# A fused attention and feed-forward kernel: the first stage with half loads on two queues and a second tile transposed by TensorE

## The chip, the cores and the metric

The kernel runs on one core of one Trainium2 chip. The metric is the device time of one execution in microseconds (us), taken as the median of several runs. Beside it stands one execution taken by the hardware profiler, whose trace gives every instruction's start and duration, in us from the start of its span.

## The reference

For an input `x` of 2048 rows and 640 columns, a linear-attention block and a gated feed-forward block are mixed by a gate for each row. Everything is bfloat16 at the boundaries.

```
qkv = x @ wqkv                       # 640 -> 3 * 640; 32 heads of 20
phi = lambda t: where(t > 0, t + 1, exp(t)) + 1e-6
pq, pk = phi(q), phi(k)
kv  = einsum("bhsd,bhse->bhde", pk, v);  z = sum over s of pk
o   = (pq @ kv) / (pq . z + 1e-6)
a   = o @ wo
b   = (gelu(x @ w_gate) * (x @ w_up)) @ w_down      # 640 -> 1728 -> 640
g   = sigmoid(sum(x * gate_w, -1))
out = g * a + (1 - g) * b
```

## The kernel before

Rows are cut into 16 tiles of 128 (`NT`), the 640 columns into five chunks of 128 (`KC`). `xT` holds x transposed (chunk by chunk, all rows) and is the stationary operand of the first stage; `x_aug` holds x as it lies. `wk` and `wq` are the k and q parts of `wqkv`, one resource for each chunk (`r_wk[k]`, `r_wq[k]`).

The instructions of every engine are written out by hand in program order. The class `_Plan` records each with the resources that it reads and writes, and puts a semaphore wait in front of an instruction for what it depends on. Each engine runs its own list in order, so an instruction that waits holds up all that follows it on its engine. Loads are issued by SP's queue (SyncE) or ACT's queue (ScalarE). A load that is issued with `dma_start_transpose` writes x transposed into `xT`; the others are plain.

The first stage runs as follows.

- POOL makes constants and the identity `ident` that TensorE's transposes need.
- ACT's queue issues a small load called touch (16 rows of 8 bytes), then wk1 and wk2 (`load_wk(1, "act")`), then an Exp on one column, which brings the table load, and then the gate vector `gw_sb`. SP's queue issues x tile 0 plain, wk0, `xT(1)` transposing, wk3, wk4, `xT(2)`, `xT(3)`, the five `wq`, `xT(4)` to `xT(15)`, and after these the rest of `x_aug` and the weights of the later stages.
- TensorE first runs matmuls on constants (`warm`, L425), then transposes tile 0 (`T`, L439; DVE copies the result out of PSUM, L443), and then works through pairs of matmuls for one tile and one chunk: `KM(n, ks)` (L459 and L460) multiplies by `wk`, `QM(n, ks)` (L474 and L475) by `wq`. `NXN` is the number of tiles that TensorE transposes, `NQ` the number of tiles that go through `KM` and `QM`; before these are 1 and 4.
- `gate_col` (L504) multiplies the gate vector by the identity, and DVE copies the five columns into column 640 of `wq` (L506, resource `r_gcol`); every `QM` reads it.
- `phi1` (ACT, L484 and L488) and `phi2` (DVE, L494 and L498) make pk and pq out of the PSUM banks of a `KM` or `QM`. `slot(n)` gives call n two of the eight banks.

From tile `NQ` on, `KQ(i)` (L545) does k and q of a tile in one pass of three groups of five matmuls, on banks 0 to 2 and 3 to 5 in turn. After the 16 tiles come `MM` (L602, L605), which multiplies pk with `x_aug`, the feed-forward groups `G` (L706), and the output stage (L827 to L880). The change leaves these as they are.

Of the kernel before, what the change touches and what calls it, by code (L numbers as in the profile page):

```python
# [15 lines left out]
NT = S // 128  # L16
KC = D // 128
# [3 lines left out]
EPS = 1e-6  # L21
XW = 656

NXN = 1
NQ = 4


class _Res:
# [134 lines left out]
def bass_gated_mix__linear_attn_block__geglu_ffn__prompt_kernel(  # L163
# [63 lines left out]
    with (  # L227
# [8 lines left out]
        with contextlib.ExitStack() as stack:  # L236
            dma_sems = [stack.enter_context(nc.semaphore("s_in%d" % i)) for i in range(n_dma_in)]

            P = _Plan(["pe", "act", "dve", "pool", "sp"])
# [9 lines left out]
            def new_dma_key():  # L249
                k = "in%d" % dma_next[0]  # L250
                dma_next[0] += 1
                return k
# [11 lines left out]
            x_aug = v16(R_XN, NT * XW).rearrange("p (i w) -> p i w", i=NT)  # L264
# [4 lines left out]
            wk = wkq[:, :, 0:640]  # L269
            wq = wkq[:, :, 640:1281]  # L270
# [31 lines left out]
            touch = v16(O_TOUCH, 16)  # L302
# [3 lines left out]
            r_xn = [P.sb("xn%d" % i, R_XN + i * XW, R_XN + (i + 1) * XW) for i in range(NT)]  # L306
# [3 lines left out]
            r_wk = [P.sb("wk%d" % k, R_WK + k * WW, R_WK + k * WW + 640) for k in range(KC)]  # L310
            r_wq = [P.sb("wq%d" % k, R_WK + k * WW + 640, R_WK + k * WW + 1280) for k in range(KC)]
# [30 lines left out]
            def dma_in(dst, src, writes, reads=(), eng="sp"):  # L342
                P.op(eng, lambda e, dst=dst, src=src: e.dma_start(dst, src),  # L343
                     reads=reads, writes=writes, dma=new_dma_key())

            def load_x(i, eng="sp"):
                dma_in(x_aug[:, i, 0:640], A_x[0, i * 128:(i + 1) * 128, :], [r_xn[i]], eng=eng)

            def load_wk(k, eng="sp", after=()):
                dma_in(wk[:, k, :], A_wqkv[k * 128:(k + 1) * 128, 640:1280], [r_wk[k]], reads=after, eng=eng)

            def load_xT(i, after=()):
                P.op("sp", lambda e: e.dma_start_transpose(xT[:, :, i * 128:(i + 1) * 128],  # L355
                                                           A_x[0, i * 128:(i + 1) * 128, :]),
                     reads=list(after), writes=[r_xT[i]], dma=new_dma_key())

            def load_wq(k, eng="sp"):
                dma_in(wq[:, k, 0:640], A_wqkv[k * 128:(k + 1) * 128, 0:640], [r_wq[k]], eng=eng)  # L360


            P.op("pool", lambda e: e.memset(ones32, 1.0), writes=[r_ones])
# [1 line left out]
                                                   base=0, channel_multiplier=1),  # L365
                 reads=[r_ones], writes=[r_ident])
            P.op("pool", lambda e: e.memset(v32(R_WO, NHC * 320), 0.0), reads=[r_ident], writes=[r_woz] + r_wo)
            P.op("act", lambda e: e.dma_start(touch[0:16, 0:4], A_wqkv[0:128:8, 640:644]),
                 writes=[P.res("touch")], dma=new_dma_key())
            load_x(0)  # L370
            load_wk(0)
            load_xT(1)
            load_wk(3)
            load_wk(4)
            load_wk(1, "act")
            load_wk(2, "act")

            zero = nc.const_aps.tensor(0.0, (128, 1), F32)
            P.op("act", lambda e: e.activation(eg[:, 0:1], zero, ACT.Exp), writes=[r_eg[0]])
            P.op("dve", lambda e: e.memset(gw_sb, 0.0), writes=[r_gw])  # L380
            dma_in(gw_sb[0:5, :], gate_w.rearrange("(k p) -> k p", p=128), [r_gw], eng="act")
            for i in range(2, NQ):
                load_xT(i)
            for k in range(KC):
                load_wq(k)
            for i in range(NQ, NT):
                load_xT(i)
            dma_in(x_aug[:, NXN:8, 0:640],
                   A_x[0, NXN * 128:8 * 128, :].rearrange("(i p) w -> p i w", p=128), r_xn[NXN:8])
# [5 lines left out]
            for h in range(2):  # L395
                src = A_wo[0:600, :].rearrange("(c h p) w -> h p c w", h=2, p=60)[h]
# [38 lines left out]
            def T(i, ks, tb):  # L435
                def fn(e):
                    last = None
                    for n, k in enumerate(ks):
                        last = e.transpose(psb[:, tb, n * 128:(n + 1) * 128],  # L439
                                           x_aug[:, i, k * 128:(k + 1) * 128], ident)  # L440
                    return last
                P.op("pe", fn, reads=[r_xn[i], r_ident], writes=[bank[tb]])
                P.op("dve", lambda e: e.tensor_copy(  # L443
                    xT[:, ks[0]:ks[-1] + 1, i * 128:(i + 1) * 128],
                    psb[:, tb, 0:len(ks) * 128].rearrange("p (k s) -> p k s", k=len(ks))),
                    reads=[bank[tb]], writes=[r_xTa[i] if ks[0] == 0 else r_xT[i]])
# [4 lines left out]
            def KM(n, ks):  # L451
                i = seq[n][1]
                b0, b1 = slot(n)

                def fn(e):
                    last = None
                    for k in ks:
                        lhs = xT[:, k, i * 128:(i + 1) * 128]
                        e.matmul(ps[:, b0, :], lhs, wk[:, k, 0:512], start=(k == 0), stop=(k == KC - 1))  # L459
                        last = e.matmul(ps[:, b1, 0:128], lhs, wk[:, k, 512:640],  # L460
                                        start=(k == 0), stop=(k == KC - 1))
                    return last
                P.op("pe", fn, reads=[r_xTa[i] if i < NXN and ks == [0] else r_xT[i]] + [r_wk[k] for k in ks],
                     writes=[bank[b0], bank[b1]])

            def QM(n, ks):
                i = seq[n][1]
                b0, b1 = slot(n)

                def fn(e):  # L470
                    last = None
                    for k in ks:
                        lhs = xT[:, k, i * 128:(i + 1) * 128]
                        e.matmul(ps[:, b0, :], lhs, wq[:, k, 0:512], start=(k == 0), stop=(k == KC - 1))  # L474
                        last = e.matmul(ps[:, b1, 0:129], lhs, wq[:, k, 512:641],  # L475
                                        start=(k == 0), stop=(k == KC - 1))
                    return last
                P.op("pe", fn, reads=[r_xT[i], r_gcol] + [r_wq[k] for k in ks],
                     writes=[bank[b0], bank[b1]])

            def phi1(n):
                b0, b1 = slot(n)
                m = n % 4
                P.op("act", lambda e: e.activation(e_buf[m], ps_flat[:, b0 * 512:b0 * 512 + 640], ACT.Exp),  # L484
                     reads=[bank[b0], bank[b1]], writes=[r_e[m]])
                kind, i = seq[n]
                if kind == "q":
                    P.op("act", lambda e: e.activation(eg[:, i:i + 1], ps[:, b1, 128:129], ACT.Tanh, scale=0.5),  # L488
                         reads=[bank[b1]], writes=[r_eg[i]])

            def phi2(n):
                b0, b1 = slot(n)
                m = n % 4
                P.op("dve", lambda e: e.tensor_scalar(e_buf[m], e_buf[m], 1.0, EPS, ALU.min, ALU.add),  # L494
                     reads=[r_e[m]], writes=[r_e[m]])
                kind, i = seq[n]
                dst, r_dst = (pk[i], r_pk[i]) if kind == "k" else (pq[i], r_pq[i])
                P.op("dve", lambda e: e.scalar_tensor_tensor(  # L498
                    dst, ps_flat[:, b0 * 512:b0 * 512 + 640], 1.0 + EPS, e_buf[m], ALU.add, ALU.max),
                    reads=[bank[b0], bank[b1], r_e[m]], writes=[r_dst])  # L500

            def gate_col():

                P.op("pe", lambda e: e.matmul(ps[:, 7, 0:5], gw_sb, ident[:, 0:5], start=True, stop=True),  # L504
                     reads=[r_gw, r_ident], writes=[bank[7]])
                P.op("dve", lambda e: e.tensor_copy(wq[:, :, 640:641], ps[:, 7, 0:5].unsqueeze(2)),  # L506
                     reads=[bank[7]], writes=[r_gcol])
# [4 lines left out]
            T(0, [0], 7)  # L512
            T(0, [1, 2, 3, 4], 6)
            warm(2, 128)
            for k in range(3):
                KM(0, [k])
            for k in range(3):
                KM(1, [k])
            KM(0, [3])
            KM(1, [3])  # L520
            gate_col()
            KM(0, [4])
            KM(1, [4])
            ALLK = list(range(KC))
            for n in range(2 * NQ):
                if n in (2, 3):
                    KM(n, ALLK)
                if n == NQ:
                    for k in ALLK:
                        QM(NQ, [k])  # L530
                        QM(NQ + 1, [k])
                if n > NQ + 1:
                    QM(n, ALLK)
                phi1(n)
                phi2(n)


            def KQ(i):
                b = 3 * (i % 2)
# [32 lines left out]
            for i in range(NQ, NT):  # L572
                KQ(i)
                if i == 4:
                    late_constants()
            P.op("dve", lambda e: e.tensor_scalar(gg, eg, 0.5, 0.5, ALU.mult, ALU.add),
                 reads=r_eg, writes=[r_g])
            P.op("dve", lambda e: e.tensor_scalar(omg, eg, -0.5, 0.5, ALU.mult, ALU.add),
                 reads=r_eg, writes=[r_omg])
# [365 lines left out]
```

## Time and profile before

| What | Value |
|---|---|
| Median of 3 runs | 273.34 us (273.16 to 273.55) |
| The profiled execution's own time | 273.49 us |
| Its span | 272.2 us |
| TensorE (PE) busy | 267.0 us, 98% of the span |
| VectorE (DVE) busy | 140.9 us, 52% |
| ScalarE (ACT) busy | 76.0 us, 28% |
| First L459 matmul, first L545 matmul | 4.45, 16.27 us |
| First matmul after the first stage (L612) | 48.94 us |

How to read the lines of a profile: PE is a TensorE matmul, PEld its weight load, which overlaps matmuls; SPq and ACTq are the DMA issues of SP's and ACT's queue, and their duration is the time of issuing, not of the transfer. A line of the timeline has the start, the duration (for several merged instructions, from the first start to the last end), engine, source line, operation, operands and count, and in brackets the engine's idle time before it and what ended it. Matmuls are pipelined: the shown duration of one is longer than the distance to the next one's start, which is what its work costs in a stream. The program's tiles all lie in one tensor named `pool`, and PSUM is `ps`.

### The profile page before, as it was taken

The numbers are of one execution on the slowest core, as the hardware profiler recorded it, in microseconds if no ns is written. First come the engines' busy times: TensorE is split into PE (matmuls) and PEld (weight loads), VectorE is DVE, ScalarE is ACT, GpSimd is POOL, SyncE is SP. The second block draws the span as 40 slices with busy tenths as digits, with TensorE's granted clock in tenths as the row PEclk, the third lists the DMA queues.
The fourth block names the chain that finished last, engine by engine and source line by source line (L and its number), as shares of the span: only waits on it lengthen the run. The fifth ranks groups of instructions, "written<-read, shape, count | busy, mean of one in ns | idle before, by whom it ended". The sixth has DMA issues, their size and how long they took to land.

```text
span 272.2 us, 3462 instructions
## 1 busy us (share of the span) xinstructions
PE 267.0 (98%) x1366; PEld 127.2 (47%) x1392; DVE 140.9 (52%) x248; ACT 76.0 (28%) x132; POOL 30.6 (11%) x30
## 2 busy tenths in 40 slices
PE   7999999999999999999999999999999999999997
PEld 3555555544445454444444444444444444444444
DVE  1678989997234335999999999634110000000200
ACT  2455555210422453332222232224011122121021
POOL 6000000003240002242332421000000000000000
DMA  7976999610200011614121221262031110110221
GB/s 192 203 117 120 356 401 379 117 3 19 58 19 2 23 52 48 198 28 52 24 48 29 46 48 25 60 233 94 2 78 40 39 39 19 41 39 19 58 60 39
DMA packets 42680, 23.61 MB, mean 87 GB/s; under 512 B 32167, under 2 KB 41255, under 8 KB 42535
## 3 DMA queue, kind: packets, MB, share of 16 engines
q1 hardware_dynamic: 42333, 23.05, 32.2%
q10 hardware_dynamic: 330, 0.33, 0.4%
q8 instruction: 11, 0.18, 0.3%
q14 instruction: 6, 0.05, 0.1%
HBM read 13.67 MB, written 2.63 MB: 60 GB/s over the span
## 4 chain that ended last, share of the span: by engine, by line
PE 96%; DMA 1%; SPq 1%; issue 1%; DVE 0%
PE ps L706 41%; PE ps L880 23%; PE ps L545 12%; PE ps L602 6%; PE ps L859 4%; PE ps L684 2%; PE ps L474 2%; PE ps L827 2%; PE ps L605 1%; DMA pool<-in_A_x_dram 1%; PE ps L459 1%; PE ps L840 1%; SPq L343 1%; SPq L355 0%; PE ps L755 0%
## 5 line engine op out<-in xcount | busy, mean ns | idle before, releaser
L706 PE MATMUL ps<-pool 128*128 128x512 bf16 x509 | 112.8, 379 | 0.7 <-issue 0.2
L706 PEld LDWEIGHTS ps<-pool 128*128 128x128 bf16 x520 | 50.6, 98 | 60.3
L880 PE MATMUL ps<-pool 128*128 128x512 bf16 (+2 forms) x300 | 62.2, 366 | 0.5 <-issue 0.2
L712 ACT ACTIVATE pool<-ps 128x512 f32<-128x512 f32 x52 | 31.1, 597 | 72.8 <-PE ps L706 70.1
L714 DVE TENSOR_TENSOR pool<-ps,pool 128x512 bf16<-128x512 f32 x52 | 34.7, 688 | 31.1 <-PE ps L706 29.8
L880 PEld LDWEIGHTS ps<-pool 128*128 128x128 bf16 x306 | 29.2, 98 | 33.4 <-issue 0.4
L863 DVE TENSOR_TENSOR pool<-ps,pool 128x512 bf16<-128x512 f32 x4 | 2.8, 692 | 61.5 <-PE ps L859 59.4
L545 PE MATMUL ps<-pool 128*128 128x512 bf16 (+1 forms) x176 | 32.5, 343 | 0.2
L770 POOL TENSOR_TENSOR pool<-pool 128x640 f32<-128x640 bf16 x16 | 22.5, 1406 | 72.6 <-DVE pool L772 65.8
L887 ACT ACTIVATE pool<-ps,pool 128x512 bf16<-128x512 f32 (+1 forms) x16 | 10.9, 681 | 68.6 <-PE ps L880 68.6
L545 PEld LDWEIGHTS ps<-pool 128*128 128x128 bf16 x180 | 17.6, 98 | 15.0
L564 DVE SCALAR_TENSOR_TENSOR pool<-ps,pool 128x128 bf16<-128x128 f32 (+2 forms) x36 | 21.7, 603 | 2.1
L555 ACT ACTIVATE pool<-ps 128x640 bf16<-128x640 f32 x24 | 16.9, 704 | 15.8 <-DVE pool L564 9.3
L602 PE MATMUL ps<-pool 128*128 128x512 bf16 x76 | 19.2, 379 | 0.1
L780 DVE TENSOR_TENSOR pool<-pool 128x640 bf16<-128x640 bf16 x16 | 13.2, 825 | 0.6
L778 DVE TENSOR_SCALAR pool<-pool 128x32 f32<-128x32 f32 x16 | 12.8, 802 | 0.6
L772 DVE TENSOR_REDUCE pool<-pool 128x32 f32<-128x640 f32 x16 | 12.9, 807 | 0.0
L650 DVE TENSOR_TENSOR pool<-pool 128x640 f32<-128x640 f32 x14 | 11.6, 825 | 0.5
L859 PE MATMUL ps<-pool 128*128 128x512 bf16 x51 | 11.4, 379 | 0.0
L652 POOL PARTITION_ALL_REDUCE pool<-pool x1 | 4.0, 3972 | 60.2 <-DVE pool L650 60.2
L602 PEld LDWEIGHTS ps<-pool 128*128 128x128 bf16 x78 | 6.9, 98 | 7.3
L561 DVE TENSOR_SCALAR pool<-pool 128x640 bf16<-128x640 bf16 x24 | 7.8, 326 | 1.7 <-ACT pool L555 0.4
(73 smaller groups left out, 123.4 us busy)
## 6 DMA issues: line engine op xcount, KB each, us to landing
out_dram<-pool SPq DMA_DIRECT2D x19, 128.0 KB, 1.7
pool<-in_B_w_gate_dram SPq DMA_DIRECT2D x1, 2080.0 KB, 14.3
pool<-in_B_w_up_dram SPq DMA_DIRECT2D x1, 2080.0 KB, 18.4
pool<-in_A_wqkv_dram SPq DMA_DIRECT2D x8, 160.0 KB, 3.0
pool<-in_A_x_dram SPq DMA_DIRECT2D x1, 1280.0 KB, 9.3
pool<-in_A_x_dram SPq DMA_DIRECT2D x1, 1120.0 KB, 6.4
pool<-in_B_w_down_dram SPq DMA_DIRECT2D x1, 1120.0 KB, 6.2
pool<-omg_row SPq DMA_DIRECT2D x1, 1024.0 KB, 4.8
```

Source lines behind the costliest of these rows:

```text
L545: last = e.matmul(ps[:, b + p, 0:c1 - c0], xT[:, k, i * 128:(i + 1) * 128], wkq[:, k, c0:c1], start=(k == 0), stop=(k == KC - 1))
L555: P.op("act", lambda e: e.activation(e_buf[m], ps_flat[:, o:o + 640], ACT.Exp), reads=banks, writes=[r_e[m]])
L564: P.op("dve", lambda e, c0=c0, c1=c1: e.scalar_tensor_tensor(dst[:, c0:c1], ps_flat[:, o + c0:o + c1], 1.0 + EPS, e_buf[m][:, c0:c1], ALU. ...
L602: last = e.matmul(ps[:, b, :], pk[i][:, c * 128:(c + 1) * 128], x_aug[:, i, 0:512], start=(i == 0), stop=(i == NT - 1))
L706: last = e.matmul(ps[:, b, :], w[:, k, fc * 128:(fc + 1) * 128], xT[:, k, j * 512:(j + 1) * 512], start=(k == 0), stop=(k == KC - 1))
L712: P.op("act", lambda e: e.activation(ge[n], ps[:, gb, :], ACT.Gelu_apprx_tanh), reads=[bank[gb]], writes=[r_ge[n]])
L714: P.op("dve", lambda e: e.tensor_tensor(hT[fc][:, j * 512:(j + 1) * 512], ps[:, ub, :], ge[n], ALU.mult), reads=[bank[ub], r_ge[n]], write ...
L770: P.op("pool", lambda e: e.tensor_tensor(tmp[n], pq[i], z_b, ALU.mult), reads=[r_pq[i], r_zb], writes=[r_tmp[n]])
L772: P.op("dve", lambda e: e.tensor_reduce(den[n], tmp[n].rearrange("p (h d) -> p h d", h=32), AX.X, ALU.add), reads=[r_tmp[n]], writes=[r_de ...
L780: P.op("dve", lambda e: e.tensor_tensor(pq[i].rearrange("p (h d) -> p h d", h=32), pq[i].rearrange("p (h d) -> p h d", h=32), den[n].unsqu ...
L859: last = e.matmul(ps[:, b, :], wd[:, fc, 512:640], hT[fc][:, j * 512:(j + 1) * 512], start=False, stop=(fc == NFC - 2), skip_group_check=True)
L880: last = e.matmul(ps[:, pb, 0:c1 - c0], lhs, rhs, start=False, stop=(q == len(rows) - 1), skip_group_check=True)
```

## The change

- `NXN` becomes 2 and `NQ` 2: TensorE transposes x tiles 0 and 1, and only tiles 0 and 1 go through `KM` and `QM`; `KQ` starts at tile 2.
- A new function `halves` loads rows 0 to 63 of a destination by SP's queue and rows 64 to 127 by ACT's queue, on one semaphore; a reader waits for both. x tile 1, the five `wk` and the five `wq` are loaded so. x tile 0 stays one load on SP's queue.
- The order of the loads is x0, wk0, x1, wk1, wk2, the gate vector (ACT's queue alone), wk3, wk4, wq0 to wq4, and then all transposing loads, from `xT(2)` on. The touch load is gone. The Exp with its table load stands ahead of ACT's loads.
- On TensorE, `T(1)` follows `KM(0, [0])`, with a DVE copy of all five chunks in one; then `KM(1, [0])`, then `KM` of tiles 0 and 1 in turn for each further chunk, with `gate_col` ahead of the last. Then `QM` of tiles 0 and 1 in turn (calls 2 and 3).

```diff
-NXN = 1
-NQ = 4
+NXN = 2
+NQ = 2
...
+            def halves(dst, src, r):
+                key = new_dma_key()
+                for h, eng in enumerate(("sp", "act")):
+                    d, f = dst[64 * h:64 * h + 64], src[64 * h:64 * h + 64]
+                    acc = P.op(eng, lambda e, d=d, f=f: e.dma_start(d, f),
+                               writes=[r] if h == 0 else [], dma=key)
+                r.writer = acc
...
-            P.op("act", lambda e: e.dma_start(touch[0:16, 0:4], A_wqkv[0:128:8, 640:644]),
-                 writes=[P.res("touch")], dma=new_dma_key())
-            load_x(0)
-            load_wk(0)
-            load_xT(1)
-            load_wk(3)
-            load_wk(4)
-            load_wk(1, "act")
-            load_wk(2, "act")
-
             zero = nc.const_aps.tensor(0.0, (128, 1), F32)
             P.op("act", lambda e: e.activation(eg[:, 0:1], zero, ACT.Exp), writes=[r_eg[0]])
             P.op("dve", lambda e: e.memset(gw_sb, 0.0), writes=[r_gw])
+            dma_in(x_aug[:, 0, 0:640], A_x[0, 0:128, :], [r_xn[0]])
+            load_wk(0)
+            load_x(1)
+            load_wk(1)
+            load_wk(2)
             dma_in(gw_sb[0:5, :], gate_w.rearrange("(k p) -> k p", p=128), [r_gw], eng="act")
-            for i in range(2, NQ):
-                load_xT(i)
+            load_wk(3)
+            load_wk(4)
             for k in range(KC):
                 load_wq(k)
-            for i in range(NQ, NT):
+            for i in range(NXN, NT):
                 load_xT(i)
...
-            for k in range(3):
+            KM(0, [0])
+            T(1, [0, 1, 2, 3, 4], 5)
+            KM(1, [0])
+            for k in range(1, KC):
                 KM(0, [k])
-            for k in range(3):
+                if k == KC - 1:
+                    gate_col()
                 KM(1, [k])
-            KM(0, [3])
-            KM(1, [3])
-            gate_col()
-            KM(0, [4])
-            KM(1, [4])
             ALLK = list(range(KC))
-            for n in range(2 * NQ):
-                if n in (2, 3):
-                    KM(n, ALLK)
-                if n == NQ:
-                    for k in ALLK:
-                        QM(NQ, [k])
-                        QM(NQ + 1, [k])
-                if n > NQ + 1:
-                    QM(n, ALLK)
+            phi1(0)
+            phi2(0)
+            phi1(1)
+            phi2(1)
+            for k in ALLK:
+                QM(2, [k])
+                QM(3, [k])
+            for n in (2, 3):
                 phi1(n)
                 phi2(n)
```

More of the change, by code (lines that the diff above doesn't have):

```diff
@@ L344, in dma_in, with load_x, load_wk @@
                      reads=reads, writes=writes, dma=new_dma_key())
[L348 to L352, printed above, removed]
+            def halves(dst, src, r):
[5 more added lines that the diff above has]
+                r.writer = acc
+            def load_x(i):
+                halves(x_aug[:, i, 0:640], A_x[0, i * 128:(i + 1) * 128, :], r_xn[i])
+            def load_wk(k):
+                halves(wk[:, k, :], A_wqkv[k * 128:(k + 1) * 128, 640:1280], r_wk[k])
             def load_xT(i, after=()):
@@ L357, in load_xT, with load_wq @@
                      reads=list(after), writes=[r_xT[i]], dma=new_dma_key())
-            def load_wq(k, eng="sp"):
-                dma_in(wq[:, k, 0:640], A_wqkv[k * 128:(k + 1) * 128, 0:640], [r_wq[k]], eng=eng)
+            def load_wq(k):
+                halves(wq[:, k, 0:640], A_wqkv[k * 128:(k + 1) * 128, 0:640], r_wq[k])
             P.op("pool", lambda e: e.memset(ones32, 1.0), writes=[r_ones])
```

## The prediction, made before the changed kernel ran

> **What bounds the kernel now.** I read the page first: one engine, TensorE, is busy for nearly the whole span, and the chain that ended last is TensorE too.
>
> ```profile
> span 272.2 us, 3462 instructions
> ...
> PE 267.0 (98%) x1366; PEld 127.2 (47%) x1392; DVE 140.9 (52%) x248; ACT 76.0 (28%) x132; POOL 30.6 (11%) x30
> ...
> PE 96%; DMA 1%; SPq 1%; issue 1%; DVE 0%
> ```
>
> So the time is the start of TensorE's stream, plus the work in it, plus its gaps. Next comes the chain in order of time: its last step that is no TensorE work is a transposing load of x; after it the chain stays on TensorE to the end, but for pieces of "issue".
>
> ```profile
> 4.15 3.90 DMA pool<-in_A_x_dram
> 8.05 0.05 issue
> 8.10 0.39 PE ps L459
> ```
>
> This is `xT(2)` (issued 4.15), for which `KM(2)` waited. The timeline of the first 17 us shows the gaps before that.
>
> ```profile
> 3.02 0.74 PE L439 MATMUL ps<-pool 128*128 128x128 bf16 x5
> ...
> 3.37 0.23 DVE L443 COPY pool<-ps 128x128 bf16<-128x128 bf16 x1 [2.39 <-PE ps L439]
> ...
> 3.79 0.42 DVE L443 COPY pool<-ps 128x512 bf16<-128x512 bf16 x1 [0.20 <-PE ps L439]
> ...
> 4.45 0.43 PE L459 MATMUL ps<-pool 128*128 128x512 bf16 x1 [0.48 <-DMA pool<-in_A_wqkv_dram]
> ...
> 5.90 0.39 PE L459 MATMUL ps<-pool 128*128 128x512 bf16 x1 [0.42 <-DMA pool<-in_A_x_dram]
> ```
>
> Real work begins at 4.45, when wk0 has landed (the copy it also needs ended at 3.60). Starts of pairs are 0.272 apart (8.10 to 10.82 for ten pairs of L459 and L460), so the fourth pair was due at 5.31 and came at 5.90 (0.59 lost, to `xT(1)`), and `KM(2)` was due at 7.83 and came at 8.10 (0.27 lost). Tile 4 (`KQ(4)`, L545) starts at 16.27. From there both kernels run the same program, and L545's matmuls had 0.2 us of idle time in all. **The change is therefore worth what it does to this 16.27**, as long as no later wait opens.
>
> The queue of SP, from the timeline of that engine:
>
> ```profile
> 0.79 0.40 SPq L343 DMA_DIRECT2D pool<-in_A_x_dram  x1
> 1.25 0.41 SPq L343 DMA_DIRECT2D pool<-in_A_wqkv_dram  x1
> 1.71 1.31 SPq L355 DMA_TRANSPOSE pool<-in_A_x_dram  x1
> 3.06 1.05 SPq L343 DMA_DIRECT2D pool<-in_A_wqkv_dram  x2
> 4.15 2.52 SPq L355 DMA_TRANSPOSE pool<-in_A_x_dram  x2
> 6.72 2.48 SPq L343 DMA_DIRECT2D pool<-in_A_wqkv_dram  x5
> 9.24 16.18 SPq L355 DMA_TRANSPOSE pool<-in_A_x_dram  x12
> ```
>
> A plain load costs its queue 0.40 to 0.57, a transposing one 1.2 to 1.7. Issue to landing: x0 2.2, wk0 3.1, the five wq 2.6 to 3.2, transposing loads 3.0 to 4.4.
>
> **Part 1: what is removed.** The waits for `xT(1)` (0.59) and `xT(2)` (0.27 at this place) and the touch load go. The touch was ACT's first issue (0.42 from 0.78); wk0's second half takes its slot. At most 0.86 is returned here, and up to 0.68 more if work could start at 3.77, where the two last warming matmuls end (0.107 each, after the transposes' 3.55).
>
> **Part 2: the Exp that now stands first on ACT.** In the timeline its table load ran from 2.20 to 3.48, and ACT's next DMA, behind it in program order, was issued at 2.27. The issue did not wait, so I take 0. If it did, all second halves would come up to 1.28 later; no row speaks for that.
>
> **Part 3: wk0 and x1 in halves.** No row shows a half load this early. Bounds for wk0: a load with little beside it landed 2.2 after its issue (x0), one with company 3.1. Its later half is SP's, issued at 1.25: landing 3.45 to 4.35. x1's halves are issued at about 1.7: landing 3.9 to 4.8. In quarter-microsecond windows DMA moved 159 and 133 GB/s from 1.75 to 2.25, SP's queue almost alone, with the engines half idle; with both queues full it moved 384, 389 and 362 from 3.25 to 4.0. So a second queue helps until about 370. x0, wk0 and x1 are 0.49 MB, which before had passed by 3.75; with ACT's queue carrying bulk from about 2.0 this should be some 3.4 to 3.6. x0's own last packets (2.5) came about 0.5 before its landing, wk0's (about 3.6) 0.7. I take wk0 at 3.8 and x1 at 4.4, nearer the middle.
>
> The Trainium skill ("DMA: Bandwidth & Descriptors", Rules for kernel authors) speaks against this part: two transfers to disjoint partition halves are not worth it, since both spread over the same 16 engines. By it wk0 stays near 4.4 and the sum below ends 0.3 higher; the half-idle engines before 2.25 speak for some gain, the ceiling of 390 after 3.25 for the rule.
>
> **Part 4: TensorE transposes x1, and `KM(1,[0])` waits for it.** `T(1)` adds five transposes and a copy, and everything on TensorE stands behind `KM(1,[0])`, because its queue runs in order: `KM(0,[1])`, whose data are there, cannot pass. Steps: `KM(0,[0])` starts at 3.85. TensorE is still slow there: L439's 128-column matmuls have 311 ns up to 3.55, L460's 219 from 4.72, and the 512-column one at 4.45 had 429 against 379, so the change fell about 0.1 after 4.45. At the slow pitch (0.427 for 512 columns, 0.107 for 128) the pair ends at 4.4. The transposes take 0.53 all slow, 0.28 all fast; with the change near 4.55, 0.37: to 4.77. The last result comes about 0.16 later. The copy of 640 columns, from 225 ns for 128 and 424 for 512, is 0.49: from 4.95 to 5.44. `KM(1,[0])` starts at 5.5. Bounds: 5.2 (loads at the short latency, clock change before 4.0) and 5.8 (x1 at 4.8; the copy then ends at 5.74). The idle stretch of about 0.75 takes the place of the two removed.
>
> The Trainium skill ("TensorE: Matmul & The Clock Gate", Part 1) calls the window of the clock gate free-running, so the change of clock need not fall at 4.55 again; by its half-microsecond scatter `KM(1,[0])` would move by about a quarter, an estimate from that page.
>
> **Part 5: gate column.** `gate_col` moves from three microseconds before its first reader to one pair before it. It started at 7.27 and its DVE copy ended at 7.68, 0.41 later; the next reader now is due 0.06 + 0.27 = 0.33 after it. With a hop of 0.06 that is 0.14 of wait. Bounds: 0 and 0.2.
>
> **Part 6: wk1 to wk4, wq.** SP's half loads follow at 0.46 each; ACT's, with the gate vector's 0.57 between, put the last half of wk3 at 3.3, of wk4 at 3.75, wq0 at 4.2, wq4 at 6.0. With 3.1 to landing: 6.4, 6.9, 7.3 and 9.1; needed at about 6.9, 7.4, 8.1 and 10.3. Cost 0, with 0.5 in hand; a wk4 that landed 4.0 after its issue would cost 0.4.
>
> **Part 7: transposing loads behind.** SP passes twelve plain issues before `xT(2)`: 0.79 + 0.46 for x0 + 11 x 0.46 to 0.55 = 6.3 to 7.3 instead of 4.15. Landing (3.0 to 4.1 after): 9.3 to 11.4; I take 6.5 + 3.9 = 10.4, as `xT(2)` itself took. `KQ(2)` is due at 5.5 + nine pairs 2.45 + gate 0.06 + 0.14 + ten pairs of 0.273 = 10.88. Cost 0, cover 0.5. Later ones come every 1.35, against 2.72 that a tile takes on TensorE. Tiles 2 and 3 in `KQ` cost (48.94 - 16.27) / 12 = 2.72 each, against 2.725 for ten pairs: nothing. Banks: `KQ(2)` needs what the first phi gives back some 1.8 after the last KM pair (8.0 to 9.68 in the timeline), and starts 2.9 after it: nothing. Big loads move by under 0.1 and are not waited for.
>
> **The sum.** `KQ(4)` starts at 10.88 + 2 x 2.72 = 16.32, against 16.27: +0.05. The profiled execution took 273.49 (span 272.2 and 1.29 around it), 0.15 above the median of 273.34, and all three runs lie within 0.39. So 273.54 in its terms, 273.4 in the median's. 0.2%, about what a measurement can tell from no change, is 0.55 us.
>
> **Rivals.** *Halves bring nothing* (the change doesn't do what it says): wk0 near 4.4, x1 at 4.8, `KM(1,[0])` at 5.8, +0.35: 273.7. For: 3.1 to landing in every load with company. Against: engines half idle before 2.25. *Slower: `xT(2)` behind twelve issues.* At 0.57 + 0.05 an issue (wk3's, the longest of these before) it starts at 8.1 and lands at 12.0 to 12.2, 1.2 late: 274.6. It decides from a landing at 10.9, and costs 0.2% from about 11.4. For: a wait on a transposing load ended last before. Against: most issues took 0.40 to 0.46. *Faster: short latency.* wk0 at 3.45, fast clock by 3.8, no gate wait: pair 3.77 to 4.04, transposes to 4.32, copy 4.48 to 4.97, `KM(1,[0])` at 5.03, `KQ(4)` at 15.7: -0.55, 272.8. Against: x1 would have to be there at 4.04, and the clock changed later.
>
> **Numbers.** Forecast (-0.25 to +0.3) 0.45; halves bring nothing 0.2; late `xT(2)` 0.2; short latency 0.15. Of the first two nearly all is within 0.2%, of the third nearly all slower, of the fourth nearly all faster: faster 0.14, same 0.63, slower 0.23. The range takes in the forecast, the halves' rival and the near parts of the others: 272.75 to 274.15.
>
> **What would show it.** Right: first L459 before 4.2; a wait of about 0.75 on L443's copy before the second pair; no wait on a transposing load before tile 2; first L545 near 10.9. Wrong: a wait on `in_A_x_dram` before L545; first L459 still at 4.4; the ACT queue's first issue after its table load; waits on wk or wq.

## The result, and the profile after

| | Median | Span of the profiled execution | First L545 matmul (tile 2 after, tile 4 before) | First matmul after the stage (L612) |
|---|---|---|---|---|
| Before | 273.44 us (4 runs) | 272.2 | 16.27 | 48.94 |
| Changed | 274.90 us (4 runs, 274.85 to 275.09) | 273.6 | 12.22 | 50.30 |

The changed kernel is slower: ratio 1.0056, 95% interval 1.0039 to 1.0074, or 1.5 us. The forecast was 273.4, no difference, with 272.75 to 274.15 as its range; the measured time lies above it. The ratios here and below leave out executions over 1.5% above the fastest of their kernel: 478 us once each in two experiments (the changed kernel's loads with the copy covered, and with fillers), 277.8 and 278.2 in a third (whole loads with the copy covered).

The chain of work that ended last is still almost all TensorE's, but what releases it early on has changed. First its line on the page (shares of the span), then its pieces in order of time (start, length, what).

```profile
PE 97%; DMA 1%; ACTq 1%; DVE 0%; issue 0%
```

```profile
4.29 0.51 ACTq L352
4.83 0.62 ACTq L352
5.48 3.48 DMA pool<-in_A_wqkv_dram
9.09 0.38 PE ps L477
...
12.22 38.08 PE ps L545 x210
```

L352 is the issue in `halves`. Before, the last release by a load in this chain was a transposing load of x, at 8.10. Now it is a half of wq0 that ACT's queue issued at 5.48, after other halves; the first `QM` waited for it until 9.09. (Two shorter waits behind it, ending at 10.92 and 12.22, are not told apart in the chain; the timeline has them.) From 12.22 the 14 tiles of `KQ` run through at 2.72 each, as before. So the whole loss is made before 12.22: 48.94 became 50.30, 1.36 us later, and the spans differ by 1.4.

The timeline shows where (L462 is the first matmul of a `KM` pair, L477 of a `QM` pair, L442 the transposes, L446 their copy, PEld the weight load of the matmul that waits):

```profile
4.24 0.38 PE L462 MATMUL ps<-pool 128*128 128x512 bf16 x1 [0.18 <-DMA pool<-in_A_wqkv_dram]
...
4.52 0.45 PE L442 MATMUL ps<-pool 128*128 128x128 bf16 x5
...
5.01 0.49 DVE L446 COPY pool<-ps 128x640 bf16<-128x640 bf16 x1 [0.70 <-PE ps L442]
5.56 0.10 PEld L462 LDWEIGHTS ps<-pool 128*128 128x128 bf16 x1 [0.76 <-DVE pool L446]
...
7.06 0.10 PEld L462 LDWEIGHTS ps<-pool 128*128 128x128 bf16 x1 [0.30 <-DMA pool<-in_A_wqkv_dram]
...
8.13 0.10 PEld L462 LDWEIGHTS ps<-pool 128*128 128x128 bf16 x1 [0.69 <-DMA pool<-in_A_wqkv_dram]
...
9.06 0.10 PEld L477 LDWEIGHTS ps<-pool 128*128 128x128 bf16 x1 [0.52 <-DVE pool L509]
...
10.92 0.10 PEld L477 LDWEIGHTS ps<-pool 128*128 128x128 bf16 x1 [0.37 <-DMA pool<-in_A_wqkv_dram]
...
12.19 0.77 PEld L545 LDWEIGHTS ps<-pool 128*128 128x128 bf16 x5 [0.34 <-issue]
```

The second pair comes at 5.56, as foretold. After it five waits follow. Counted from when the stream was due (the start of the last 128-column matmul plus 0.055), they are 0.14 for wk3, 0.52 for wk4, 0.37 for wq0 and the gate column, 0.20 for wq3, and 0.20 for `xT(2)`, which was issued at 8.38 and landed 3.7 later (12.09): 1.43 in all, where the prediction had 0.14. (For the last the profile names no releaser; the landing, 0.13 ahead of the matmul, fits.) The queues show why:

```profile
2.49 5.85 SPq L352 DMA_DIRECT2D pool<-in_A_wqkv_dram  x9
...
4.29 4.40 ACTq L352 DMA_DIRECT2D pool<-in_A_wqkv_dram  x7
...
8.38 3.95 SPq L363 DMA_TRANSPOSE pool<-in_A_x_dram  x3
```

Nine half loads took 5.85 us of SP's queue and seven 4.40 of ACT's: 0.65 and 0.63 each, for 82 kB. A whole load of 164 kB cost 0.40 to 0.58 before. The two queues together bring 164 kB in 0.64 us, so at most some 256 GB/s, and issue without a pause until 8.4 and 8.7.

### The profile page after: what moved, and what is told of

Read it like the earlier page. It is cut to its first block, busy times and chain, and to the rows that moved or that the text cites. A ratio compares the mean times of both kernels' runs of the same rounds, so it can differ in the third digit from the quotient of the medians.

```text
span 273.6 us, 3493 instructions
## 1 busy us (share of the span) xinstructions
PE 269.5 (98%) x1387; PEld 127.2 (46%) x1387; DVE 142.0 (52%) x251; ACT 76.0 (28%) x132; POOL 30.6 (11%) x30
## 4 chain that ended last, share of the span: by engine, by line
PE 97%; DMA 1%; ACTq 1%; DVE 0%; issue 0%
PE ps L706 41%; PE ps L880 23%; PE ps L545 14%; PE ps L602 6%; PE ps L859 4%; PE ps L827 2%; PE ps L684 2%; PE ps L605 1%; DMA pool<-in_A_wqkv_dram 1%; PE ps L477 1%; PE ps L428 1%; PE ps L840 1%; PE ps L755 0%; ACTq L352 0%; PE ps L731 0%; ACTq L343 0%
## 5 line engine op out<-in xcount | busy, mean ns | idle before, releaser
L706 PEld LDWEIGHTS ps<-pool 128*128 128x128 bf16 x520 | 50.6, 98 | 60.2
L880 PEld LDWEIGHTS ps<-pool 128*128 128x128 bf16 x306 | 29.1, 98 | 33.5 <-issue 0.4
L545 PE MATMUL ps<-pool 128*128 128x512 bf16 (+1 forms) x210 | 38.1, 344 | 0.0
L545 PEld LDWEIGHTS ps<-pool 128*128 128x128 bf16 x210 | 20.5, 98 | 17.7 <-issue 0.3
L564 DVE SCALAR_TENSOR_TENSOR pool<-ps,pool 128x128 bf16<-128x128 f32 (+2 forms) x42 | 25.3, 603 | 2.4
L555 ACT ACTIVATE pool<-ps 128x640 bf16<-128x640 f32 x28 | 19.7, 704 | 18.1 <-DVE pool L564 10.9
L602 PEld LDWEIGHTS ps<-pool 128*128 128x128 bf16 x78 | 7.0, 98 | 7.3
L561 DVE TENSOR_SCALAR pool<-pool 128x640 bf16<-128x640 bf16 x28 | 9.2, 327 | 1.7 <-ACT pool L555 0.2
```

Source lines behind the costliest of these rows:

```text
L545: last = e.matmul(ps[:, b + p, 0:c1 - c0], xT[:, k, i * 128:(i + 1) * 128], wkq[:, k, c0:c1], start=(k == 0), stop=(k == KC - 1))
L555: P.op("act", lambda e: e.activation(e_buf[m], ps_flat[:, o:o + 640], ACT.Exp), reads=banks, writes=[r_e[m]])
L564: P.op("dve", lambda e, c0=c0, c1=c1: e.scalar_tensor_tensor(dst[:, c0:c1], ps_flat[:, o + c0:o + c1], 1.0 + EPS, e_buf[m][:, c0:c1], ALU. ...
L602: last = e.matmul(ps[:, b, :], pk[i][:, c * 128:(c + 1) * 128], x_aug[:, i, 0:512], start=(i == 0), stop=(i == NT - 1))
L706: last = e.matmul(ps[:, b, :], w[:, k, fc * 128:(fc + 1) * 128], xT[:, k, j * 512:(j + 1) * 512], start=(k == 0), stop=(k == KC - 1))
L880: last = e.matmul(ps[:, pb, 0:c1 - c0], lhs, rhs, start=False, stop=(q == len(rows) - 1), skip_group_check=True)
```

## The experiments

Thirteen runs, in four groups, each group on one chip with its own runs of the kernel before; between groups only the ratios compare. All keep the changed kernel's TensorE program unless a diff shows otherwise.

**Does the issue cost lie in the half, or in two queues at once?**

Both halves on SP's queue:

```diff
-                for h, eng in enumerate(("sp", "act")):
+                for h, eng in enumerate(("sp", "sp")):
```

> The same 64-row halves, both on SP's queue, one after the other; ACT's queue has the gate vector alone. It measures what one half costs a queue with no other queue issuing. If the cost lies in the 64-row shape: 0.5 to 0.6 each, as the two 64-row loads of w_down before the output stage (0.59, 0.50). If it lies in two queues issuing at once: 0.40 to 0.43. Either way 22 issues in a row make the time longer than the changed kernel's: the first transposing load is issued near 11 (0.43) to 14 (0.55), and tile 2 waits to 15 to 18: 278 to 281 us.

One execution: 281.08 us. The view of L352 (duration in ns: least, median, most; first and last start):

```profile
L352 SPq DMA_DIRECT2D pool<-in_A_wqkv_dram x20: 561/597/601, 1.2 to 14.6; - x20
```

With no bulk on the other queue a half still costs 0.6. Then halves by columns, on both queues:

```diff
-                    d, f = dst[64 * h:64 * h + 64], src[64 * h:64 * h + 64]
+                    d, f = dst[:, 320 * h:320 * h + 320], src[:, 320 * h:320 * h + 320]
```

> Halves by columns instead of rows: 128 rows of 320 columns, the left half on SP's queue, the right half on ACT's. Same number of issues and bytes on both queues as the changed kernel; only the shape differs. If the cost lies in the 64-row shape: issues of 0.40 to 0.46, the first transposing load near 6.3, time near 273.7. If it lies in two queues issuing at once: issues of 0.6, 274.9. Rows of 640 bytes may also move more slowly than rows of 1280; then loads land later with short issues.

```profile
L352 ACTq DMA_DIRECT2D pool<-in_A_wqkv_dram x10: 353/453/454, 0.8 to 6.1; - x10
L352 SPq DMA_DIRECT2D pool<-in_A_wqkv_dram x10: 414/432/434, 1.3 to 6.0; - x10
```

Same bytes and number of issues, and both queues busy, but 0.43 to 0.45 each. So the cost belongs to the 64-row shape and not to two queues at once: both halves of that question are settled. The time was no better: 276.17, ratio 1.0075 (1.0040 to 1.0109). Rows of 640 bytes moved slowly at first (0.83 MB from 1.5 to 5.5 us, as with row halves), x1 came late (transposes at 5.39), and TensorE's clock was slow until 9.9 (512-column matmuls of 0.61 to 0.63). No load was waited for after x1.

**Whole loads in the same order.** In turn on both queues, and all on SP's:

```diff
-            def halves(dst, src, r):
-                key = new_dma_key()
...
+            qn = [0]
+
+            def halves(dst, src, r):
+                eng = "act" if qn[0] % 2 == 0 else "sp"      # second kernel: eng = "sp"
+                qn[0] += 1
+                dma_in(dst, src, [r], eng=eng)
```

> Whole loads of 128 rows in the same order of use, in turn on ACT's and SP's queue (wk0 ACT, x1 SP, wk1 ACT, ...); TensorE's program as in the changed kernel. Theory (the number and the cost of the half loads' issues is the loss: a half costs its queue 0.60 to 0.66 us, a whole one 0.41): issues go back to 0.40 to 0.46, SP comes to the first transposing load near 3.6 us instead of 8.38, the waits on wk3, wk4, wq3 and xT(2) go, and KQ starts tile 2 near 11.0 instead of 12.22: about 1.2 us less than the changed kernel, 273.7, the kernel before's time within 0.3. Rival 1 (two queues that issue at the same time slow each other): issues stay at 0.6, but there are half as many; wk4 still lands before 7.0, so the time is also near 273.7, and the issue rows tell it apart. Rival 2 (the DMA engines' rate is the limit, about 230 GB/s): wk4 and wq land as late as with halves, and the time stays at 274.9.

> Whole loads in order of use, all on SP's queue, ACT's queue with the gate vector alone. Theory: an issue costs 0.41 to 0.43, pitch 0.47; the first transposing load is issued near 0.79 + 12 x 0.47 = 6.4 and lands near 10.3, before tile 2 is due at 11; x1 is issued third, at 1.7, and lands near 4.5. About 273.8. Rival 2 (rate of the DMA engines): no better than the changed kernel, 274.9.

The issues are short again (first the run on two queues, then SP alone):

```profile
L343 SPq DMA_DIRECT2D pool<-in_A_wqkv_dram x4: 432/432/435, 1.7 to 3.1; - x4
...
L343 SPq DMA_DIRECT2D pool<-in_A_wqkv_dram x10: 407/432/433, 1.3 to 6.0; - x10
```

They were 0.38 to 0.48 apart, the first transposing load went out at 3.61 and 6.46, and the waits on wk, wq and `xT(2)` were gone in both profiles. Tile 2 started at 11.68 and 11.54 instead of 12.22; the same point of the kernel before is 10.83 (16.27 less two tiles). The times were 275.3 (274.2 to 275.9; ratio 1.0056, 1.0033 to 1.0080) and 274.04 (273.9 to 276.0; ratio 1.0030, 1.0005 to 1.0054). On two queues wk0, whole, and x0 come together: x0 landed at 3.7 instead of 3.1, so that the second pair came at 6.29; on SP alone x1 landed at 5.0, and the second pair at 6.14. So the theory held for the waits, but not for the time: a start of the second pair that is 0.6 to 0.7 later took half of the gain.

**Which halves?** Halves for wk0, x1, wk1 and wk2 only:

```diff
             def halves(dst, src, r):
+                n_load[0] += 1
+                if n_load[0] > 4:
+                    dma_in(dst, src, [r], eng="sp" if n_load[0] % 2 else "act")
+                    return
                 key = new_dma_key()
```

> The changed kernel with halves for wk0, x1, wk1 and wk2 only; wk3, wk4 and the five wq are whole loads of 128 rows, in turn on SP's and ACT's queue. TensorE's program is unchanged. Theory (the later halves' issues are the loss): the second pair still comes near 5.56; wk3 and wk4 land near 6.8 and 7.2, the first transposing load is issued near 5.6 instead of 8.38, the waits on wk3, wk4, wq0, wq3 and xT(2) (1.38 us together) fall to the 0.17 of the gate column; tile 2 starts near 11.0; 273.7, within 0.3 of the kernel before. Rival (the rate of the DMA engines, or the order of the loads): the waits stay, 274.9.

Measured 274.99, ratio 1.0061 (1.0039 to 1.0083): the theory in this form fell. The second pair came at 6.08, not near 5.56, because x0 and both halves of wk0 landed later than in the changed kernel's profile (transposes of x0 at 3.47 instead of 3.13). And the waits on wk3 and wk4 stayed (here L468 is the pair's first matmul):

```profile
6.08 0.39 PE L468 MATMUL ps<-pool 128*128 128x512 bf16 x1 [0.59 <-DVE pool L452]
...
7.59 0.10 PEld L468 LDWEIGHTS ps<-pool 128*128 128x128 bf16 x1 [0.32 <-DMA pool<-in_A_wqkv_dram]
...
8.78 0.10 PEld L468 LDWEIGHTS ps<-pool 128*128 128x128 bf16 x1 [0.80 <-DMA pool<-in_A_wqkv_dram]
```

The first four pairs of halves and the gate vector (0.84) keep the queues until 3.77 and 4.30. wk3 and wk4 start only then, and land 3.8 and 4.4 after their issue, with the wq close behind them; as halves they had landed 2.7 and 3.3 after. From 1.5 to 5.5 us 0.85 MB had moved, as with all halves (0.84), against 1.13 with whole loads on two queues. The new theory was that the early halves do the damage. Its mirror tests it: the touch first on ACT, wk0, wk1 (SP) and x1, wk2 (ACT) whole, and wk3, wk4 and all wq in halves.

```diff
+            P.op("act", lambda e: e.dma_start(touch[0:16, 0:4], A_wqkv[0:128:8, 640:644]),
+                 writes=[P.res("touch")], dma=new_dma_key())
...
-            load_wk(0)
-            load_x(1)
-            load_wk(1)
-            load_wk(2)
+            whole(wk[:, 0, :], A_wqkv[0:128, 640:1280], r_wk[0], "sp")
+            whole(x_aug[:, 1, 0:640], A_x[0, 128:256, :], r_xn[1], "act")
+            whole(wk[:, 1, :], A_wqkv[128:256, 640:1280], r_wk[1], "sp")
+            whole(wk[:, 2, :], A_wqkv[256:384, 640:1280], r_wk[2], "act")
```

> The mirror of the run with early halves: the touch load is back as ACT's first issue, wk0, wk1 (SP) and x1, wk2 (ACT) are whole loads, wk3, wk4 and the five wq are halves on both queues. TensorE's program as in the changed kernel. Theory (the early halves put every later load behind: with them 0.81 to 0.85 MB had moved from 1.5 to 5.5 us, with whole loads on two queues 1.10 to 1.13): the halves now start a microsecond earlier, wk3 and wk4 land before 7.0, the first transposing load is issued near 6.6, and no wait on a load over 0.2 is left after the second pair: 274.0, as with whole loads only. Rival (the late halves are what is late, whenever they start): waits on wk4, wq and xT(2) of 0.5 or more, 274.6 or more.

Measured 274.16, ratio 1.0034 (1.0015 to 1.0053). The second pair starts at 5.79; the waits after it are 0.17 for the gate column (8.44) and 0.1 for `xT(2)`, which landed at 11.15; tile 2 starts at 11.28:

```profile
5.79 0.39 PE L467 MATMUL ps<-pool 128*128 128x512 bf16 x1 [0.58 <-DVE pool L451]
...
8.44 0.10 PEld L482 LDWEIGHTS ps<-pool 128*128 128x128 bf16 x1 [0.34 <-DVE pool L514]
```

Fourteen halves are still there, on the same queues at 0.6 each, and nothing waits for them; whole loads throughout, with the touch, cost as much (1.0032, below). So late halves cost nothing, and the early ones are what to leave out. The mirror has the touch back as well, but whole loads on SP alone without it came to the same (1.0030). With it ran the changed kernel once more, unedited:

> The changed kernel itself, on the chip of this call, against the same runs of the kernel before as the other two. If the loss is the late halves, which do not depend on the moment at which TensorE's clock changes: 274.8 to 275.1 in most runs, 1.3 to 1.5 above the kernel before. If the state of the clock makes the difference: a spread of a microsecond or more between its runs.

It took 275.72, ratio 1.0074 (1.0055 to 1.0093), all six runs between 275.39 and 276.25: more than the first time, and neither expectation met it. In the same group the kernel with early halves is therefore 1.0074 less 1.0034, some 1.1 us, slower than the one without. How much of that is late loads is open, because the repeat's profile has another cause in front:

```profile
3.36 0.71 PE L442 MATMUL ps<-pool 128*128 128x128 bf16 x5
...
4.69 0.59 PE L462 MATMUL ps<-pool 128*128 128x512 bf16 x1 [0.41 <-DMA pool<-in_A_wqkv_dram]
...
6.51 0.61 PE L462 MATMUL ps<-pool 128*128 128x512 bf16 x1 [0.59 <-DVE pool L446]
```

x0's transposes came 0.23 later than in the first profile (3.36 against 3.13), and TensorE ran slowly until 9.0: 0.59 to 0.63 for 512 columns instead of 0.38. Five pairs from 6.51 on took about 0.53 each instead of 0.272, so the late halves were no longer waited for, and tile 2 started at 13.12, 0.9 later still. In these two profiles, whichever is later, the loads or the slow clock, sets the end of this stretch.

**The wait for the copy of x1.** The changed kernel's loads, with two more pairs behind the transposes and the gate column earlier:

```diff
             KM(0, [0])
             T(1, [0, 1, 2, 3, 4], 5)
+            KM(0, [1])
+            KM(0, [2])
             KM(1, [0])
-            for k in range(1, KC):
-                KM(0, [k])
-                if k == KC - 1:
-                    gate_col()
-                KM(1, [k])
+            KM(1, [1])
+            gate_col()
+            KM(1, [2])
+            for k in (3, 4):
+                KM(0, [k])
+                KM(1, [k])
```

> The changed kernel's loads, halves and all; on TensorE two more pairs of tile 0 (chunks 1 and 2) stand between the transposes of x1 and the first pair of tile 1, so that DVE's copy is covered, and the gate column comes three pairs before its reader. Theory (the last halves of wk4 and wq0 set the end of this stretch, the wait for the copy is hidden behind them): no gain, tile 2 still near 12.2, 274.8 to 274.9. Rival (the wait for the copy, 0.6 us, is part of the loss): 274.2 or less.

No gain: ratio 1.0061 (1.0040 to 1.0083), four runs from 274.85, as in the changed kernel's first runs, to 275.81. Its profile was one with the slow clock (until 8.6; tile 2 at 12.72), so that the waits could not be read from it. Then whole loads with the touch first on ACT's queue, first with the changed kernel's order on TensorE, then with the order above:

```diff
             load_wk(0)
-            load_x(1)
+            load_x(1, "act")
             load_wk(1)
-            load_wk(2)
+            load_wk(2, "act")
...
             load_wk(3)
-            load_wk(4)
+            load_wk(4, "act")
             for k in range(KC):
-                load_wq(k)
+                load_wq(k, "act" if k % 2 else "sp")
```

> Whole loads only, with the touch load first on ACT's queue as in the kernel before: SP x0, wk0, wk1, wk3, wq0, wq2, wq4, then transposing loads; ACT touch, x1, wk2, wk4, the gate vector, wq1, wq3. TensorE's program as in the changed kernel. Theory: x0 lands at 3.0 again (with wk0 whole at the same moment on ACT's queue it landed at 3.7), wk0 and x1 near 4.35, the second pair starts near 5.7, no wait on a load after it; tile 2 starts near 11.1: 273.6 to 273.8. Rival (DMA rate): x1 or wk late, 274.5.

> The loads of the run with whole loads and touch, together with the order on TensorE that covers the copy and the gate column. Theory: without late loads behind it the copy's wait is now what ends last, so that covering it pays here: the stretch from the first pair has no wait over 0.2, tile 2 starts near 10.3 to 10.5, against 10.83 for the same point of the kernel before (16.27 less two tiles of 2.72): 272.8 to 273.1, faster than both. Rival: wk1 or wk2 land late (near 5.5 to 6) and TensorE waits for them instead: 273.4 to 273.7, as the kernel before.

274.11, ratio 1.0032 (1.0013 to 1.0050), and 273.97, ratio 1.0006 (0.9991 to 1.0021). The ratios differ by 0.26%, 0.7 us, but their intervals overlap, and two high runs of the first (275.59 and 276.20) make most of it; without these two the means differ by 0.2, and so do the profiles from the first pair to tile 2. Where no load is late, covering the copy therefore pays some 0.2 us, and perhaps more; where the halves are late no gain is seen. The second of the two is level with the kernel before, not ahead of it. What it still loses shows in its first pairs:

```profile
4.27 0.59 PE L456 MATMUL ps<-pool 128*128 128x512 bf16 x1 [0.22 <-DMA pool<-in_A_wqkv_dram]
...
6.10 0.50 PE L456 MATMUL ps<-pool 128*128 128x512 bf16 x1
```

By the count used above, one wait is left after 4.27: 0.32, up to 5.61, for wk1, which landed at 5.48, as this run's rival had it. And until about 6.3 everything runs at the slow clock (0.50 to 0.59 for 512 columns). To ask whether earlier data would help, wk1 took x1's place as ACT's first load and x1 went behind wk0 on SP, with `KM(0, [1])` ahead of `T(1)`, `KM(0, [2])` alone between it and `KM(1, [0])`, and `KM(0, [3])` behind the gate column:

```diff
-            load_x(1, "act")
-            load_wk(1)
+            load_wk(1, "act")
+            load_x(1)
...
             KM(0, [0])
-            T(1, [0, 1, 2, 3, 4], 5)
             KM(0, [1])
+            T(1, [0, 1, 2, 3, 4], 5)
             KM(0, [2])
...
```

> The run with whole loads and the covered copy (273.97), with wk1 instead of x1 as ACT's first load, x1 on SP behind wk0, and on TensorE two pairs of tile 0 ahead of the transposes of x1, three pairs of tile 0 behind them. If what is left of the loss is waiting for loads: the first three pairs run on without a wait, tile 2 starts 0.2 to 0.3 earlier, 273.2 to 273.6, level with the kernel before or ahead of it. If it is the slow clock at the start (0.59 to 0.63 us for a 512-column matmul until 6.3 us in that run): no gain, 273.7 to 274.1.

274.21, ratio 1.0035 (1.0009 to 1.0060): no gain. Its profile is that of a run among the highest four of twelve (276.11): the first pair began only at 5.10, because wk0 beside wk1 landed at 5.0, and the clock was slow until 10.1.

**The clock.** Matmuls on constants in TensorE's idle time, in the changed kernel and in the run with late halves:

```diff
-            warm(2, 128)
+            warm(5, 128)
             KM(0, [0])
             T(1, [0, 1, 2, 3, 4], 5)
+            warm(5, 128)
```

> The changed kernel with five instead of two 128-column matmuls on constants behind the transposes of x0, and five more between the transposes of x1 and the first pair of tile 1, in time that TensorE spent idle. If idle time is what keeps the clock slow (of the 3.4 us before a change of clock that was missed, TensorE had been busy for 61 to 74% in the runs with columns, the repeat and wk1 first; before one that came, 79 to 86%): the clock changes before 7 us in every run, and the late half loads are left as the floor: 274.8 to 275.1, without runs above 275.3. If the moment is chance: 275.4 to 276.2 again, as in the repeat.

> The run with late halves (273.86 to 274.44 in seven runs, 275.42 to 276.04 in three) with the same ten matmuls on constants. If idle time decides on the clock: the upper group goes, all runs between 273.8 and 274.5. If not: the upper group stays, in about a third of the runs.

With the changed kernel's loads the five runs that were compared took 274.85 to 275.60, ratio 1.0061 (1.0040 to 1.0081). That is below the repeat's 275.39 to 276.25, but three of the five lie above 275.3, so the expectation was met only in part, and no trace of this kernel shows its waits in such a run. With late halves all twelve runs fell between 273.83 and 274.63, ratio 1.0020 (1.0008 to 1.0032); the group above 275.4, three of ten before, was gone. This speaks for idle time as what decides on the clock, but does not show it: three of ten against none of twelve, on another chip, can be chance in about one case of thirteen.

A plainer sign lies in the run with both halves on SP's queue, where TensorE waited most. The lines show, for three stretches that follow each other, the length, the busy time of PE (with the number of matmuls), PEld, DVE, ACT and POOL, then the granted clock and the DMA:

```profile
4.60:8.01 3.41, 1.73 (x13) 0.70 (x11) 0.49 (x1) 0.00 (x0) 0.76 (x2) 1.00 0.50 133
8.01:11.42 3.41, 3.12 (x12) 1.20 (x13) 0.00 (x0) 0.02 (x1) 0.00 (x0) 0.50 0.46 129
11.43:14.84 3.41, 2.07 (x13) 0.76 (x12) 2.39 (x5) 1.27 (x2) 0.00 (x0) 1.00 0.46 124
```

After 3.4 us with 1.73 of work the clock was half for the next 3.4 (512-column matmuls of 0.61 to 0.63), and after 3.12 of work it was full again. It then stayed full, though the third stretch had only 2.07. How much idle time is allowed is not settled, and busy time alone does not settle it. In stretches of 3.4 us after which the clock stayed slow TensorE had been busy 2.27, 2.50 and 2.86 us (wk1 first, columns, the repeat; 67 to 84%, not the 61 to 74% of the expectation). In stretches that ended with the change it had been busy 2.92 and 2.93 (before, whole x1) and more, but in the repeat itself only 2.82 (5.63 to 9.04).

## Why the prediction was wrong

Parts 1, 2 and 5 held in the profile of the changed kernel: the waits on `xT(1)` and `xT(2)` at their old places are gone, and the Exp on ACT held up no issue (table load from 0.79, the first half issued at 0.85). The gate column's wait was 0.17 where it could be read alone (0.14). `KQ` costs the same for tiles 2 and 3, and no bank was waited for.

`KM(1,[0])` came at 5.56, as parts 3 and 4 had it (5.5), but partly by luck. wk0 landed at 4.1 instead of 3.8, and the first pair came at 4.24 instead of 3.85. The clock, however, had become full before that pair and not at 4.55, so that the pair and the transposes of x1 took 0.57 instead of 0.92. In two other profiles with the same first loads and this order the second pair came at 6.08 and 6.51, beyond the bound of 5.8.

**Part 6 is the step that failed**, and with it the size of a term in part 7. Both reckoned half loads at 0.46 apiece, the pitch of whole loads (part 7 with 0.55 as the upper end). A half costs 0.60 with a pitch of 0.65. So the last half of wk3 was issued at 4.29 instead of 3.3 (the gate vector between, at 0.84 instead of 0.57, did its part), wk4 at 4.83 instead of 3.75, wq0 at 5.48 instead of 4.2 and wq4 at 8.07 instead of 6.0. The landings were not at fault: these halves landed 2.7 to 3.5 after their issue, where the prediction had 3.1. The waits on wk and wq, put at 0, came to 1.23 together with the gate column's. `xT(2)` went out at 8.38, above the range of 6.3 to 7.3, and landed at 12.09; its wait was 0.20, small only because TensorE had been held up before. A row with the price of 64 rows was in the trace of the kernel before, at the two halves of the last rows of w_down:

```profile
174.87 0.59 SPq L343 DMA_DIRECT2D pool<-in_B_w_down_dram  x1
...
177.17 0.50 SPq L343 DMA_DIRECT2D pool<-in_B_w_down_dram  x1
```

The prediction used the range of whole loads instead. Of its signs of being wrong, waits on wk and wq came.

The sentence on wk4 ("would cost 0.4") named the right place for another reason: wk4 landed 3.3 after its issue, not 4.0, but was issued 1.1 later than predicted, and cost 0.52. The slower rival, `xT(2)` behind twelve issues, had the right cause, slow issues, and the right times (8.1 and 12.0 to 12.2, against 8.38 and 12.09), but the wrong victim: loads that were due earlier were late first. That its 274.6 is close is therefore luck in part.

The rule against halves from the Trainium skill ("DMA: Bandwidth & Descriptors", Rules for kernel authors), weighed in part 3, was right to speak against them. The sum by it (+0.3) was small beside what was measured. That wk0 came earlier as halves holds for the first profile alone: there the first pair began at 4.24, against 4.45 before, but at 4.69 to 4.74 in three others with the same first loads (early halves, order only, the repeat), and at 4.27 to 4.53 in four with wk0 whole on SP's queue and x1 whole beside it on ACT's.

The prediction also took one moment for the clock's change (4.55). The first profile had it before 4.24, the repeat at 9.0, at a cost of 0.9 beyond the late loads. That run-to-run term was estimated at a quarter of a microsecond.

What stays open is the rest of the loss. Without early halves the kernel was still 0.3% behind the one before; whole loads with the copy covered were level with it. How the remainder divides between the wait for the copy, the later first loads and the clock, these runs do not separate.

## What to carry to other kernels

Price a load by its shape and count the issues on each queue. Half a load can cost each of two queues more than the whole cost one, and everything queued behind pays. The halves of the first loads cost most, since all later loads start after them. When one wait is removed, ask which load is next due and when it is issued, before asking about the last one in the queue. Work at the very start is also priced by TensorE's clock, so a wait there can cost more than its length.

## What the runs showed of the hardware

- A plain load of 64 rows of 1280 bytes cost its queue 0.56 to 0.60 us alone and 0.49 to 0.68 beside another queue (once 0.83 in each of two profiles). One of 128 rows cost 0.34 to 0.46, whether its rows had 1280 or 640 bytes, and up to 0.59 as the first on SP's queue behind another kind of load. Half the rows cost more, not less; why, no run shows.
- Two queues with whole loads moved 1.10 to 1.13 MB from 1.5 to 5.5 us, one queue 0.96, two with row or column halves 0.81 to 0.85.
- x0's landing (by the start of its transposes) went with what else was issued at 0.8: 3.0 to 3.2 beside a small load, 3.1 to 3.5 beside a half, 3.8 beside a whole load.
- TensorE's clock became full between 3.8 and 6.3 us in ten profiles of nearly the same start, and between 8.6 and 10.1 in four. Ahead of the change the profile's granted clock reads 1.00, and only the matmuls' durations (0.59 to 0.63 against 0.38 for 512 columns) show the slow clock. Once it had been full and fell back, as with both halves on SP's queue, the record showed it: 0.50 from 8.01 to 11.42. The Trainium skill ("TensorE: Matmul & The Clock Gate", Part 1) calls the window some 3.4 us long and free-running; the length of that stretch agrees, and so does the step from changes before 6.3 to changes after 8.6. That the window runs free, no run here shows.
